# Decode attention and MLP: K and V in items of 32 pairs with a running maximum, instead of items of one KV head

## The chip, the core and the metric

The kernel runs on one core of one Trainium2 chip. The metric is the time of one execution on the device in microseconds (us). The core has five engines that run side by side, each with its own in-order instruction queue: TensorE (PE in the profile; its weight loads are PEld) does matrix products into PSUM, VectorE (DVE) and ScalarE (ACT) do elementwise work, reductions and 32x32 block transposes, GpSimd (POOL) does slower elementwise work, and SyncE (SP) issues transfers. Sixteen DMA engines carry the transfers from HBM into SBUF, the memory with 128 partitions from which the engines work.

## The reference

One token for each of 8 sequences goes through sliding-window attention and through an MLP, and a gate mixes both. With B = 8, D = 576, 32 query heads, 16 KV heads, head size 128, a cache of 8192 positions and a window of the last W = 2048:

```python
q = (x @ wq)                                   # (8, 32 heads, 128)
k = k_cache[:, :, Sk - W:, :]; v = v_cache[:, :, Sk - W:, :]   # each KV head serves 2 query heads
scores = einsum("bhqd,bhkd->bhqk", q, k) * Dh ** -0.5
a = einsum("bhqk,bhkd->bhqd", softmax(scores), v) @ wo
b = gelu(layernorm(x) @ w1 + b1) @ w2 + b2     # hidden size 4608
g = sigmoid((x * gate_w).sum(-1))
out = g * a + (1 - g) * b
```

All data are bf16. K and V of the window are 2 x 67 MB, which is most of what is read (154 MB); there are 128 pairs of sequence and KV head, and of each pair the window is 512 KB of K and 512 KB of V, contiguous.

## The kernel before

The kernel is written as a list of operations, each with an engine, its dependencies, an estimated cost and a priority. A small planner (class _Plan) simulates them with these costs and fixes from that the order on every engine; then each engine's instructions are emitted in that order, with semaphore waits for the dependencies. So an operation whose input is late holds up everything behind it on its engine.

Loading. Everything that is large is loaded on SP's queue in one order: wq and w1, then the entries of the list named stream, K0, K1, K2, V0, K3, V1 and so on up to V15, with a quarter of wo after every fourth V; then b2 and w2. SBUF has four slots of 32 KB a partition for K, V and w2, used in turn (take_slot: 1, 2, 0, 3), and half a slot more for wo. A load waits until the slot's earlier content has been read: for K the transposes, for V the weighted sum. The waits stand on SP in the order of the stream.

An item is one KV head of all 8 sequences, 4 MB (load_item). Its window is cut in 32 pieces of 64 positions; a row of 16 KB is one piece of one sequence, and a partition gets two rows.

Scores. For each item k_unit runs four times: a transpose of 128 x 2048 float32 on DVE (named tr, L647), which turns positions and head elements within 32x32 blocks (two bf16 at a time), into one of two KT buffers; then eight matmuls on PE (named qk, L659 and L175; one weight load serves four of them). A transpose waits for the qk that read its buffer two steps earlier. The weights qbd hold the query block-diagonally, and PSUM banks 0 to 3 collect the scores of two items, a group; there are eight groups. Entries that belong to no query are set to a large negative value beforehand (mask, L629, on ACT).

Softmax. Once per group: maximum over the scores (mx, L620, DVE), its combination over partitions (a tiny matmul, L622, and nb, L623), exp into P (L624, ACT, which also sums), the mask for the next group, transpose of P (pt, L631, DVE), and the sum's reciprocal through another tiny matmul.

Weighted sum. v_item issues 32 matmuls for an item (pv, L681): 32 columns of weights from the transposed P, 512 columns of V, two at a time in different column strips of the array. After each second item the result is masked and folded on DVE (vmul, acc), spread on POOL (ew), summed over partitions on PE (us), scaled on ACT (oev) and, after four items, transposed on DVE (oT). A projection with a quarter of wo follows on PE as soon as its chunk is there (class AccGroup, L563).

MLP and end. The hidden layer is computed at the start, beside the first K loads; its product with w2 comes last, in parts of 12, 12, 8, 3 and 1 rows of 128, with a few matmuls on zeros in between (keep_warm, L715). Then the accumulator is copied out by DVE and ACT (L777, L778) and stored.

Of the kernel before, what the change touches and what calls it, by code (L numbers as in the profile page):

```python
# [181 lines left out]
def build_kernel(nc, A_x, A_k_cache, A_v_cache, A_wq, A_wo, B_x, B_w1, B_b1, B_w2, B_b2, gate_w, out):  # L182
# [9 lines left out]
    HG = 2  # L192
    NG = Hkv // HG
# [16 lines left out]
    with ExitStack() as es:  # L210
# [20 lines left out]
        req("iqm", 32, F32)  # L231
        req("maskr", 4, F32)
        req("maskq", 4, F32)
        req("maskv", 4, F32)
        req("kq", 128, F32)
        req("selv", 128, F32)
        req("seln", 128, F32)
# [18 lines left out]
        req("sm", 32 * NG, F32)  # L256
        req("gcol", 1, F32)
        req("rr", 2, F32)
        req("on", 256, BF)
        req("EW", 512, F32)  # L260
        req("EV", 2 * 128, F32)
        req("oT", NG * 128, BF)
# [5 lines left out]
        over("vm", "uh", 0, 512, F32)  # L268
# [39 lines left out]
        iqm, maskr, selv = view("iqm"), view("maskr"), view("selv")  # L308
        maskq, maskv, kq = view("maskq"), view("maskv"), view("kq")
# [6 lines left out]
        qbd = view("qbd").rearrange("p (u h m) -> p u h m", u=4, h=4)  # L316
# [7 lines left out]
        sm = view("sm").rearrange("p (g k) -> p g k", g=NG)  # L324
        gcol = view("gcol")
        rr = view("rr")
        on = view("on")
        maskhd = view("maskhd")
        EW = view("EW").rearrange("p (g h d) -> p g h d", g=2, h=2)
        oT = view("oT").rearrange("p (i j c) -> p i j c", i=NG // 2, j=WOR)  # L330
        seln = view("seln")
# [4 lines left out]
        EV = view("EV").rearrange("p (u n) -> p u n", u=2)  # L336
        RAW = view("RAW")
        x_sb, gw_sb, y_bf = view("x_sb", 8), view("gw_sb", 8), view("y_bf", 8)
# [5 lines left out]
        def slot(s):  # L344
            return RAW[:, s * DE:min((s + 1) * DE, ND * DE + SE)]

# [21 lines left out]
        dma_keys = ["x", "b", "b2", "wq", "w1", "out"] + ["s%d" % i for i in range(ND + 1)] + ["t%d" % i for i in range(5)]  # L368
# [16 lines left out]
        o_mR = add("pool", lambda e: e.affine_select(out=maskR, in_=ones_bf, pattern=[[0, 128], [1, 4]], compare_op=ALU.is_equal,  # L385
                                                     fill=0.0, base=0, channel_multiplier=-1), deps=[o_ones], name="maskR", cost=0.8, prio=-1)
        o_mL = add("pool", lambda e: e.affine_select(out=maskL, in_=zeros_bf, pattern=[[0, 16], [1, 4], [0, 2]], compare_op=ALU.is_equal,
# [71 lines left out]
        o_iqm = add("dve", lambda e: e.tensor_reduce(out=iqm.rearrange("p (q m) -> p q m", q=4), in_=ident.rearrange("p (q r m) -> p q m r", q=4, r=4), axis=AXL.X, op=ALU.add), deps=[o_ident, o_obl], name="iqm", cost=0.3, prio=-1)  # L459
        o_maskr = add("dve", lambda e: e.tensor_reduce(out=maskr, in_=i32.rearrange("p (r m) -> p r m", r=4), axis=AXL.X, op=ALU.add), deps=o_i32, name="maskr", cost=0.2, prio=-1)  # L460
        o_maskq = add("dve", lambda e: e.tensor_reduce(out=maskq, in_=ident.rearrange("p (q m) -> p q m", q=4), axis=AXL.X, op=ALU.add), deps=[o_ident, o_xT], name="maskq", cost=0.3)
        o_kq = add("pool", lambda e: e.tensor_copy(kq.rearrange("p (q m) -> p q m", q=4), bass.AP(arena_f, offset=foffs("i32"), ap=[[AST // 2, 128], [0, 4], [1, 32]])), deps=o_i32, name="kq", cost=0.3, prio=-1)
        o_maskhd = add("dve", lambda e: e.tensor_reduce(out=maskhd, in_=iqm.rearrange("p (n h) -> p h n", h=2), axis=AXL.X, op=ALU.add), deps=[o_iqm], name="maskhd", cost=0.2, prio=-1)

        def seln_fn(e):
            dst = bass.AP(arena_f, offset=foffs("seln"), ap=[[AST // 2, 128], [32, 4], [8, 4], [1, 8]])
            src = bass.AP(arena_f, offset=foffs("i32"), ap=[[AST // 2, 128], [8, 4], [0, 4], [1, 8]])
            return e.tensor_copy(dst, src)
        o_seln = [add("pool", seln_fn, deps=o_i32, name="seln", cost=0.3, prio=-1)]
        o_selv = []  # L470
        for l in range(4):
            def selv_fn(e, l=l):
# [166 lines left out]
        def k_unit(i, s, d):  # L639
# [28 lines left out]
            if q == 3:  # L668
                softmax(g)
# [164 lines left out]
```

## Time and profile before

| what | value |
|---|---|
| median of 3 runs | 365.83 us (365.74 to 366.01) |
| profiled execution: its own time | 366.32 us |
| profiled execution: span, first to last instruction | 364.9 us |
| busy: PE, PEld, DVE, ACT, POOL | 247.1, 57.3, 217.0, 39.9, 23.3 us |
| mean granted TensorE clock | 0.846 |
| read from HBM | 154.31 MB, mean 423 GB/s over the span |
| time of the 16 DMA engines taken by SP's queue | 99.1% |

The page gives busy time per engine, the span in 40 slices of 9.1 us, the DMA queues, the chain of work that ended last (followed back from the last instruction to what released it), groups of instructions by source line, and transfers. In a line of the groups, "xN | busy us, mean ns | idle" means N instructions, their busy time, the mean of one, and how long the engine stood idle just before them with what ended that. Matmuls overlap, so their means are longer than their spacing. The granted clock is the share of full speed at which TensorE was allowed to run; it is either 1.0 or 0.5, in stretches that are multiples of 3.41 us.

### The profile page before, as it was taken

How to read it: one execution, taken by the hardware profiler on the slowest of the kernel's cores; microseconds unless marked ns; L12 is line 12 of the kernel's file. 1: busy time of each engine (PE TensorE's matmuls, PEld its weight loads, DVE VectorE, ACT ScalarE, POOL GpSimd, SP SyncE). 2: the span in 40 equal slices, each digit the busy share in tenths (PEclk: the TensorE clock that was granted, in tenths of full speed). 3: DMA queues.
4: the chain of work that ended last, by engine and by line, in shares of the span. 5: the costliest groups of instructions: out<-in, count | busy, mean ns of one | idle time of the engine just before them, and what ended most of it. 6: DMA issues, size and time to landing. Idle time of an engine off the chain costs nothing.

```text
span 364.9 us, 2626 instructions
## 1 busy us (share of the span) xinstructions
PE 247.1 (68%) x1347; PEld 57.3 (16%) x893; DVE 217.0 (59%) x160; ACT 39.9 (11%) x46; POOL 23.3 (6%) x66
## 2 busy tenths in 40 slices
PE   0355676599486957849297957868396938587776
PEld 0100000122111121202111121202110210102333
DVE  0723999667883757256675657276756667085220
ACT  1012100400310040000400040000400040001100
POOL 7210001000100000001000100001000100000000
PEclk9986599699769986969768986989589968969699
DMA  8999999999999999999999999999999999999996
GB/s 347 432 408 429 431 433 427 408 429 432 429 431 431 436 427 431 433 431 433 428 431 433 424 433 429 431 435 431 433 429 433 433 431 429 431 431 431 426 428 263
DMA packets 10674, 154.47 MB, mean 423 GB/s; under 512 B 764, under 2 KB 932, under 8 KB 1320
## 3 DMA queue, kind: packets, MB, share of 16 engines
q1 hardware_dynamic: 10608, 154.29, 99.1%
q8 instruction: 8, 0.13, 0.1%
q10 hardware_dynamic: 56, 0.03, 0.0%
q14 instruction: 2, 0.02, 0.0%
HBM read 154.31 MB, written 0.01 MB: 423 GB/s over the span
## 4 chain that ended last, share of the span: by engine, by line
DMA 66%; DVE 21%; PE 10%; issue 1%; ACT 1%; SPq 0%; DVEq 0%
DMA arena<-in_A_k_cache_dram 59%; DVE arena L647 20%; DMA arena<-in_B_w_dram 7%; PE ps L175 5%; PE ps L659 2%; PE ps L681 2%; DVE arena L546 1%; DVE arena L620 1%; ACT ps L629 1%; PE ps L563 0%; DVE arena L545 0%; PE ps L633 0%; DVE arena L777 0%; PE ps L622 0%; SPq L406 0%
## 5 line engine op out<-in xcount | busy, mean ns | idle before, releaser
L647 DVE STREAM_TRANSPOSE arena<-arena 128x2048 f32<-128x2048 f32 x64 | 144.1, 2289 | 61.8 <-DMA arena<-in_A_k_cache_dram 40.6
L175 PE MATMUL ps<-arena 128*128 128x512 bf16 (+2 forms) x454 | 135.0, 449 | 0.0
L659 PE MATMUL ps<-arena 128*128 128x512 bf16 x128 | 57.7, 451 | 52.5 <-DVE arena L647 52.5
L681 PE MATMUL ps<-arena 128*32 128x512 bf16 x512 | 60.3, 390 | 2.6 <-DVE arena L635 1.9
L624 ACT ACTIVATE arena<-ps,arena 128x2048 bf16<-128x2048 f32 x8 | 15.7, 1967 | 240.5 <-DVE arena L623 240.5
L659 PEld LDWEIGHTS ps<-arena 128*128 128x128 bf16 x128 | 14.0, 109 | 171.9 <-DVE arena L647 114.6
L681 PEld LDWEIGHTS ps<-arena 128*32 128x32 bf16 x512 | 25.2, 99 | 46.1 <-issue 20.3
L620 DVE TENSOR_REDUCE arena<-ps 128x1 f32<-128x2048 f32 x8 | 18.3, 2287 | 12.5 <-PE ps L175 12.4
L614 POOL COPY arena<-arena 32x128 bf16<-32x128 bf16 x32 | 9.2, 288 | 211.3 <-PE ps L175 201.5
L631 DVE STREAM_TRANSPOSE arena<-arena 128x2048 bf16<-128x2048 bf16 x8 | 18.3, 2292 | 6.4 <-ACT arena L624 6.4
L691 DVE SCALAR_TENSOR_TENSOR arena<-ps,arena 128x512 f32<-128x512 f32 x8 | 6.0, 751 | 19.8 <-PE ps L681 19.8
L563 PE MATMUL ps<-arena 128*8 128x288 bf16 (+1 forms) x140 | 12.6, 339 | 6.9 <-DVE arena L706 5.6
L700 PE MATMUL ps<-arena 128*128 128x256 f32 x16 | 5.8, 444 | 16.0 <-POOL arena L696 16.0
L633 PE MATMUL ps<-arena 128*128 128x1 f32 x16 | 4.6, 359 | 15.0 <-ACT ps L629 14.2
L629 ACT ACTIVATE ps<-arena 128x2048 f32<-128x2048 f32 x7 | 13.1, 1876 | 0.1
L696 POOL TENSOR_TENSOR arena<-arena 128x256 f32<-128x256 f32 x8 | 4.9, 612 | 111.3 <-DVE arena L623 63.3
L438 PE MATMUL ps<-arena 8*128 8x8 bf16 x8 | 0.6, 171 | 14.7 <-DVE arena L412 9.6
L694 DVE TENSOR_REDUCE arena<-arena 128x128 f32<-128x512 f32 x8 | 8.4, 1048 | 0.3
L563 PEld LDWEIGHTS ps<-arena 128*8 128x8 bf16 (+1 forms) x140 | 6.4, 97 | 13.5 <-DVE arena L706 7.0
L703 ACT ACTIVATE arena<-ps,arena 64x256 bf16<-64x256 f32 x8 | 3.7, 465 | 43.1 <-PE ps L700 43.1
L706 DVE STREAM_TRANSPOSE arena<-arena 128x256 bf16<-128x256 bf16 x4 | 2.5, 634 | 9.8 <-ACT arena L703 9.8
L541 DVE TENSOR_TENSOR arena<-arena 128x1152 f32<-128x1152 f32 x1 | 1.4, 1359 | 10.5 <-ACT arena L539 10.5
(88 smaller groups left out, 66.2 us busy)
## 6 DMA issues: line engine op xcount, KB each, us to landing
arena<-in_A_k_cache_dram SPq DMA_DIRECT2D x16, 4096.0 KB, 28.1
arena<-in_A_v_cache_dram SPq DMA_DIRECT2D x16, 4096.0 KB, 33.0
arena<-in_B_w_dram SPq DMA_DIRECT2D x1, 4608.0 KB, 23.4
arena<-in_A_wo_dram SPq DMA_DIRECT2D x4, 1152.0 KB, 34.7
arena<-in_A_wq_dram SPq DMA_DIRECT2D x1, 4096.0 KB, 13.0
arena<-in_B_w_dram SPq DMA_DIRECT2D x2, 1728.0 KB, 27.3
arena<-in_B_w_dram SPq DMA_DIRECT2D x1, 1152.0 KB, 26.7
arena<-in_B_w_dram SPq DMA_DIRECT2D x1, 576.0 KB, 24.3
```

The costliest lines, as they stand in the source:

```text
L175: return e.add_instruction(mybir.InstMatmult(name=nc.get_next_instruction_name(), engine=mybir.EngineType.PE, ins=[e.lower_ap(rhs), e.lowe ...
L563: ins = e.matmul(ps[32 * j:32 * j + 8, BK_ACC, 0:JN], lhsT, rhs[:, JN * j:JN * j + JN], start=False, stop=True, skip_group_check=True, til ...
L614: return e.tensor_copy(dst, src)
L620: mx = add("dve", lambda e: e.tensor_reduce(out=k(MX), in_=ps[:, 0:4, :].rearrange("p a n -> p (a n)"), axis=AXL.X, op=ALU.max), deps=[qk_ ...
L624: ex = add("act", lambda e: e.activation(out=Pm, in_=ps[:, 0:4, :].rearrange("p a n -> p (a n)"), func=ACTF.Exp, bias=k(NB), scale=SCALE, ...
L629: mask_done[g + 1] = add("act", lambda e: e.activation(out=ps[:, 0:4, :].rearrange("p a (n c) -> p (a n) c", c=4), in_=bass.AP(arena_f, of ...
L631: pt_done[g] = add("dve", lambda e: e.transpose(bass.AP(arena, offset=aoffs("PT") + 2048 * (g % 2), ap=[[AST, 128], [8, 64], [512, 4], [1, ...
L647: tr = add("dve", (lambda h=h, kb=kb: lambda e: e.transpose(bass.AP(arena_f, offset=foffs("KT") + kb * 2048, ap=[[AST // 2, 128], [1, 2048]]),
L659: mm = e.matmul(*args, start=False, stop=True, skip_group_check=True) if rc == 0 else held_matmul(nc, e, *args, stop=True, skip=True)
L681: mm = e.matmul(ps[c:c + 32, BK_OS[g % 2], :], PT[:, g % 2, 16 * c + 32 * t:16 * c + 32 * t + 32], slot(s)[:, (j % 2) * SE + 512 * t:(j % ...
L691: vmul = add("dve", lambda e: e.scalar_tensor_tensor(out=vmv, in0=ps[:, BK_OS[g % 2], :].rearrange("p (r d) -> p r d", r=4), scalar=rr[:, ...
L694: acc_ev[g] = add("dve", lambda e: e.tensor_reduce(out=EV[:, g % 2, :], in_=vm.rearrange("p (r d) -> p d r", r=4), axis=AXL.X, op=ALU.add) ...
```

## The change

An item is now a quarter of the window (512 positions) of 32 pairs of sequence and KV head, again 4 MB. The 512 positions of a pair are four rows of 32 KB that follow each other in HBM, and each partition gets one row. Four items make a group g of 32 pairs; there are four groups and 16 items n, as many as before.

- Softmax runs for every item, so 16 times instead of 8, with a maximum that runs over the four items of a group: nb takes the smaller of its own bound and the earlier one's, al is the factor by which earlier results shrink, ss the running sum. The scores of an item fill the four PSUM banks, and the mask is written for each. The combination over partitions is done once a group (sw, nbq, wt, rc, cf).
- For the weighted sum the transposed P is spread into a buffer with four diagonal blocks (ptx, 16 KB a partition, in the place of the half slot): four copies per item (qrx), two on POOL and two on ACT, and for the last item one on POOL, two on ACT, one on DVE. The buffer is cleared once (ptx0). Then 64 matmuls with 128 columns of weights and 256 columns of V run per item, after the scores of the next item in PE's order. There is one ptx buffer, so the copies of an item wait for the weighted sum of the item before.
- The result of an item is added to O on DVE (o): O = O x al + new. After the fourth item come vmul, acc, ew and us; oev and oT come once, at the very end.
- The stream is K0, K1, V0, K2, V1 and so on. All of wo is loaded after the last V, behind the first half of w2, and all of the projection follows it. The keep-warm matmuls are no longer called.
- Before the items, the masks and selection matrices are built in other shapes by small DVE and POOL instructions; the query copies on ACT are four of 256 elements instead of eight of 128.

The diff, cut to what the text speaks of (lines marked with - are the kernel before, those marked with + the new one):

```diff
-        NVW = Hkv // (Hq // WO_CH)
-        stream = [("K", 0), ("K", 1), ("K", 2)]
-        for vi in range(Hkv):
+        stream = [("K", 0), ("K", 1)]
+        for vi in range(NL):
             stream.append(("V", vi))
-            if (vi + 1) % NVW == 0:
...
+            if vi + 2 < NL:
+                stream.append(("K", vi + 2))
...
-        stream += [("B", 0)] + [("M", i) for i in range(len(M_CUTS))]
+        stream += [("B", 0), ("M", 0), ("W", 0), ("M", 1)]
 
...
-        slot_free = [[o_qp], [], [], [o_hp], [o_qp, o_hp]]
+        slot_free = [[o_qp], [], [], [o_hp]]
+        o_px0 = add("pool", lambda e: e.memset(ptx_f, 0.0), deps=[o_qp, o_hp], name="ptx0", cost=4.5)
...
-        def load_item(cache, nm, hkv):
+        def load_item(cache, nm, n):
             s = take_slot()
-            src = cache[:, hkv, S0:Sk, :].rearrange("b (x r) d -> x b (r d)", x=32)
-            d = dma("sp", lambda e: e.dma_start(slot(s).rearrange("p (u n) -> p u n", u=2), src), "s%d" % s, 8 * W * Dh * 2, deps=slot_free[s], name="%s%d" % (nm, hkv), after=last_dma[-1:])
+            g, i = divmod(n, 4)
+            src = cache.rearrange("b h s d -> (b h) s d")[32 * g:32 * g + 32, S0 + KL * i:S0 + KL * i + KL, :].rearrange("j (x r) d -> j x (r d)", x=4)
+            d = dma("sp", lambda e: e.dma_start(slot(s), src), "s%d" % s, 8 * W * Dh * 2, deps=slot_free[s], name="%s%d" % (nm, n), after=last_dma[-1:])
             last_dma.append(d)
...
+            mx = add("dve", lambda e: e.tensor_reduce(out=k(n, MX), in_=ps[:, 0:4, :].rearrange("p a n -> p (a n)"), axis=AXL.X, op=ALU.max), deps=[qk_unit[n]], name="mx%d" % n, cost=2.25, prio=5)
+            if i == 0:
+                nb = add("dve", lambda e: e.tensor_scalar(out=k(n, NB), in0=k(n, MX), scalar1=-SCALE, scalar2=None, op0=ALU.mult), deps=[mx], name="nb%d" % n, cost=0.16, prio=5)
+            else:
+                nb = add("dve", lambda e: e.scalar_tensor_tensor(out=k(n, NB), in0=k(n, MX), scalar=-SCALE, in1=k(n - 1, NB), op0=ALU.mult, op1=ALU.min), deps=[mx, nb_done[n - 1]], name="nb%d" % n, cost=0.16, prio=5)
...
+            ex = add("act", lambda e: e.activation(out=Pm, in_=ps[:, 0:4, :].rearrange("p a n -> p (a n)"), func=ACTF.Exp, bias=k(n, NB), scale=SCALE, accum_out=k(n, S)),
+                     deps=[nb, pt_done[n - 1] if n else o_zz], name="exp%d" % n, cost=1.95, prio=5)
...
+            if n + 1 < NL:
+                mask_done[n + 1] = add("act", lambda e: e.activation(out=ps[:, 0:4, :].rearrange("p a (n c) -> p (a n) c", c=32), in_=bass.AP(arena_f, offset=foffs("maskv"), ap=[[AST // 2, 128], [0, 64], [1, 32]]), func=ACTF.Copy),
+                                       deps=[ex], name="mask%d" % (n + 1), cost=1.85, prio=4)
...
+            pt_done[n] = add("dve", lambda e: e.transpose(bass.AP(arena, offset=aoffs("PT") + 2048 * (n % 2), ap=[[AST, 128], [1, 2048]]), Pm),
+                             deps=[ex] + (px_done[n - 2] if n >= 2 else [o_yTp, o_hT]), name="pt%d" % n, cost=2.3, prio=5)
+            if i:
+                al_done[n] = add("act", lambda e: e.activation(out=k(n, AL), in_=k(n - 1, NB), func=ACTF.Exp, bias=k(n, NB), scale=-1.0), deps=[nb], name="al%d" % n, cost=0.25, prio=4)
+                ss_done[n] = add("dve", lambda e: e.scalar_tensor_tensor(out=k(n, SS), in0=k(n - 1, SS if i > 1 else S), scalar=k(n, AL), in1=k(n, S), op0=ALU.mult, op1=ALU.add),
+                                 deps=[ex, al_done[n], ss_done.get(n - 1)], name="ss%d" % n, cost=0.16, prio=3)
...
+                sw_pe = add("pe", lambda e: e.matmul(ps[:, BK_S, 4:5], swp, k(n, NB), start=True, stop=True), deps=[nb, o_u] + o_swp + prev, name="sw_pe%d" % g, cost=0.5, prio=3)
+                nbq = add("dve", lambda e: e.tensor_tensor(out=G(NBQ), in0=k(n, NB), in1=ps[:, BK_S, 4:5], op=ALU.min), deps=[sw_pe], name="nbq%d" % g, cost=0.16, prio=3)
...
+                sw = add("dve", lambda e: e.tensor_tensor(out=G(SW), in0=k(n, SS), in1=G(WT), op=ALU.mult), deps=[wt, ss_done[n]], name="sw%d" % g, cost=0.16, prio=3)
+                su = add("pe", lambda e: e.matmul(ps[:, BK_S, 0:1], pair, G(SW), start=True, stop=True), deps=[sw, o_pair] + prev, name="sum_pe%d" % g, cost=0.5, prio=3)
+                rc = add("dve", lambda e: e.reciprocal(out=G(RC), in_=ps[:, BK_S, 0:1]), deps=[su], name="rc%d" % g, cost=0.16, prio=3)
+                cf = add("dve", lambda e: e.tensor_tensor(out=G(CF), in0=G(WT), in1=G(RC), op=ALU.mult), deps=[rc], name="cf%d" % g, cost=0.16, prio=3)
+                grp_done[g] = [nbq, rc, cf]
...
+                    m = 4 * n + 2 * rh + hh
+                    kb = m % 2
+                    deps = [d] + ([qk_half[m - 2]] if m >= 2 else [o_selp])
+                    tr = add("dve", (lambda rh=rh, hh=hh, kb=kb: lambda e: e.transpose(bass.AP(arena_f, offset=foffs("KT") + kb * 2048, ap=[[AST // 2, 128], [1, 2048]]),
...
+            qk_unit[n] = qk
...
+            softmax(n)
...
+        def v_item(n):
+            s, d = load_item(A_v_cache, "dv", n)
...
+            ob_ = BK_OS[n % 2]
+            px_done[n] = []
+            for c in range(4):
+                def fn(e, c=c):
+                    dst = bass.AP(arena, offset=32 * c * AST + PX + 32 * c, ap=[[AST, 32], [128, 64], [1, 32]])
...
+                    if px_engs[n][c] == "act":
+                        return e.activation(out=dst, in_=src, func=ACTF.Copy)
+                    return e.tensor_copy(dst, src)
+                px_done[n].append(add(px_engs[n][c], fn, deps=[pt_done[n], pv_done.get(n - 1), o_px0], name="qrx%d_%d" % (n, c), cost={"act": 1.8, "dve": 2.2, "pool": 4.0}[px_engs[n][c]], prio=5))
...
             def pv_fn(e):
                 mm = None
-                for t in range(16):
-                    for j in (i - 1, i):
-                        c = 32 * (j % 4)
-                        mm = e.matmul(ps[c:c + 32, BK_OS[g % 2], :], PT[:, g % 2, 16 * c + 32 * t:16 * c + 32 * t + 32], slot(s)[:, (j % 2) * SE + 512 * t:(j % 2) * SE + 512 * t + 512],
-                                      start=(t == 0), stop=(t == 15), skip_group_check=True, tile_position=(0, c))
+                for r in range(64):
+                    rhs = bass.AP(arena, offset=aoffs("RAW") + s * DE + 128 * r, ap=[[AST, 128], [SE, 2], [1, 128]])
+                    mm = e.matmul(ps[:, ob_, 0:256], ptx[:, r, :], rhs, start=(r == 0), stop=(r == 63), skip_group_check=True)
                 return mm
...
+            deps = [d, o_u] + px_done[n] + [o_done.get(n - 2)]
+            pv = add("pe", pv_fn, deps=deps, name="pv%d" % n, cost=7.2, after=pv_hist[-1:] + [qk_unit.get(n + 1)])
...
+            if i == 0:
+                o_done[n] = add("dve", lambda e: e.tensor_copy(Oc, ps[:, ob_, 0:256]), deps=[pv, acc_done.get(g - 1)], name="o%d" % n, cost=0.4, prio=6)
+            else:
+                o_done[n] = add("dve", lambda e: e.scalar_tensor_tensor(out=Oc, in0=Oc, scalar=al, in1=ps[:, ob_, 0:256], op0=ALU.mult, op1=ALU.add), deps=[pv, al_done[n], o_done[n - 1]], name="o%d" % n, cost=0.5, prio=6)
+            if i == 3:
+                vmv = vm.rearrange("p (r d) -> p r d", r=2)
...
+                           deps=[o_done[n], o_maskrh, o_hf] + grp_done[g], name="vmul%d" % g, cost=0.5, prio=6)
...
+        def wo_all(_):
+            def place(s, at, i):
+                dst = slot(s)[:, at:at + WO_CH * D]
+                h0 = WO_CH * i
+                d = dma("sp", lambda e: e.dma_start(dst, A_wo[128 * h0:128 * (h0 + WO_CH), :].rearrange("(p j) c -> p (j c)", j=WOR)),
+                        "o%d" % i, WO_CH * 128 * D * 2, deps=slot_free[s] if at == 0 else [], name="d_wo%d" % i, after=last_dma[-1:])
+                last_dma.append(d)
+                dj = dst.rearrange("p (j c) -> p j c", j=WOR)
+                return AccGroup("proj%d" % i, [(oT[:, j, i, :], dj[:, j, :]) for j in range(WOR)], o_T + [d], cost=1.0, prio=1).op
+            s = take_slot()
+            done = [place(s, WO_CH * D * i, i) for i in range(3)]
+            slot_free[s] = done
+            s = take_slot()
+            done = [place(s, 0, 3)]
+            m2_at.append((s, WO_CH * D))
+            slot_free[s] = done
+
+        m2_at = []
         o_m2 = []
 
```

## The prediction

> **What bounds the kernel now.** Of the page I read the slices and queues first, then the chain, then the groups; after that the chain in order of time, and windows of the TensorE clock.
>
> ```profile
> GB/s 347 432 408 429 431 433 427 408 429 432 429 431 431 436 427 431 433 431 433 428 431 433 424 433 429 431 435 431 433 429 433 433 431 429 431 431 431 426 428 263
> ...
> q1 hardware_dynamic: 10608, 154.29, 99.1%
> ...
> DMA 66%; DVE 21%; PE 10%; issue 1%; ACT 1%; SPq 0%; DVEq 0%
> ...
> L647 DVE STREAM_TRANSPOSE arena<-arena 128x2048 f32<-128x2048 f32 x64 | 144.1, 2289 | 61.8 <-DMA arena<-in_A_k_cache_dram 40.6
> ...
> L681 PE MATMUL ps<-arena 128*32 128x512 bf16 x512 | 60.3, 390 | 2.6 <-DVE arena L635 1.9
> L624 ACT ACTIVATE arena<-ps,arena 128x2048 bf16<-128x2048 f32 x8 | 15.7, 1967 | 240.5 <-DVE arena L623 240.5
> ...
> L620 DVE TENSOR_REDUCE arena<-ps 128x1 f32<-128x2048 f32 x8 | 18.3, 2287 | 12.5 <-PE ps L175 12.4
> ```
> The transfers are the bound: the queue is 99.1% busy at about 431 GB/s, and the transposes wait for K (40.6 us). So 4.19 MB take 9.73 us and a pair (one K and one V transfer) 19.45. The question is whether the engines still fit under 19.45 us a pair. What one step takes, from the chain in order of time and a timeline of TensorE:
>
> ```profile
> 37.31 2.31 DVE arena L647
> ...
> 49.63 8.79 DVE arena L647 x4
> ...
> 68.51 0.45 PE ps L659
> 68.96 1.28 PE ps L175 x3
> ...
> 78.61 0.22 PE ps L659
> 78.84 0.69 PE ps L175 x3
> ...
> 361.26 1.73 PE ps L563 x24
> ```
> ```profile
> 23.19 0.61 PE L510 MATMUL ps<-arena 128*128 128x256 bf16 x4 [2.60 <-DVE arena L504]
> ```
> Four transposes in a row take 8.8 to 9.0. One weight load and four matmuls of 512 columns take 1.71 at half clock and 0.91 at full clock. Four pairs of weight load and 256-column matmul took 0.61 with a mean of 275 ns each: (610 - 275) / 3 = 112 ns apart at full clock. The windows are 3.41 us long; columns are PE busy, count, granted clock, DMA share, GB/s:
>
> ```profile
> 116.42:119.83 3.41, 1.82 (x8) 1.00 0.95 408
> ...
> 194.93:198.34 3.41, 1.67 (x8) 1.00 1.04 447
> 198.34:201.75 3.41, 3.17 (x8) 0.56 1.01 432
> 201.75:205.17 3.42, 2.92 (x13) 0.94 0.97 414
> ...
> 297.32:300.74 3.42, 1.77 (x14) 0.50 1.01 431
> 300.74:304.15 3.41, 2.59 (x7) 0.50 1.00 428
> 304.15:307.56 3.41, 2.81 (x12) 0.94 0.98 413
> ```
> A window with 1.67 busy is followed by half clock, one with 1.82 was not; a half-clock window with 2.59 busy ends it, one with 1.77 does not. About half a window decides.
>
> **The change, part by part.** Transfers: same bytes. In windows of the trace the 32 KB rows of wq run at 428 GB/s (4 to 14 us), the 36 KB rows of w1 at 438 (16 to 24 us), the 16 KB rows of K and V at 431 (100 to 300 us). For the 134 MB of K and V that is between 2.2 us lost and 5.0 gained; I take 0, as wq's rows have the new size. The rows now come from 32 pairs 2 MiB apart; no row of this trace has such a pitch, and it is a rival below. Every K item now has its own maximum, exp, mask and transpose of P, where two items shared one of each: on DVE that adds 8 x (2.29 + 2.29) = 37 us. The weighted sum has 64 matmuls of 256 columns an item with full 128-column weights, for 32 of 512 that ran two at a time (3.56 us in the chain). A pair then has DVE 9.0 + 2.29 + 2.29 + some 0.9 = 14.5, ACT 2.16 + 1.88 + 0.2 + two spreading copies (at most 1.97 each, as exp) = 8.2, PE 32 x 0.227 + 64 x 0.112 = 14.4. None fills 19.45; the order does it.
>
> In the changed program's order DVE runs, per pair n: four transposes, mx, nb, pt, o(n-1), ss, then the transposes of n+1. PE runs the four halves qk(n), then all of pv(n-1). So o(n-1) stands ahead of the next transposes and waits for a weighted sum that starts only after the last qk. Nothing of this depends on a transfer once K and V lie in their slots. The ring: transposes 9.0, last half 0.05 + 1.98 (8 x 0.227 and the drain), pv 64 x 0.112 + 0.2 = 7.35, o about 0.5 (0.75 for 512 columns), ss 0.17, gaps 0.15: 19.2 at full clock. The other branch, mx 2.29, nb 0.25, exp 2.2, pt 2.3, is 7.05 instead of 7.35, hidden by pv. pv could also pay its weight load whole: 112 + 109 = 221 ns each, 14.1 us; I take 112, since that row is the same pair of instructions.
>
> Each group of four adds the normalisation: sw, rc, cf between transposes (0.5), nbq (0.2), vmul and acc (0.4 + 0.6) ahead of the transposes: 1.7.
>
> The clock: from pv's end to the next qk, PE idles for o, ss and the first transpose, 3.1 us. Wherever the windows' edges fall, one holds nearly 1.55 us of idleness or more; unless the edge splits the gap almost evenly (0.3 of 3.41) busy is under 1.7 and half clock follows for one window of qk. A half then takes 3.4 instead of 1.8, and the transpose that needs its buffer waits: first half 2.3 to 5.7, third transpose to 8.0, fourth to 10.2, last half done at 12.2, against 11.0. So about 1.0 a pair, with bounds 0 and 2.2 (two halves at half clock).
>
> By the Trainium skill (TensorE: Matmul & The Clock Gate, Part 1), half clock comes back after a whole idle window of about 3.4 us; 3.1 us would not trip it, and the ring would stay at its full-clock sum, the second rival below. The windows differ: 1.67 busy was already too little.
>
> Start: K0 lands at 37.3 as before and its transposes end at 49.6, with the MLP's DVE work between. Then mx0 to 54.2, exp 56.6, mask 58.6. PE has idled 7 us, so qk(1) starts cold: K1's third and fourth transposes end at 64.3 and 67.7, qk(1) at 69.7, pv(0) at 77.0. Here the order takes the next first transpose ahead of pt, which saves 2.3 and the PE gap: K2's other three start at 77.8, K3's at 94.9. The first of K4 starts at 112.3, and K4 has landed at 47.0 + 3 x 19.45 = 105.4: 7 us behind.
>
> From K4 to K15: 11 periods of 19.2 = 211.2; groups 3 x 1.5 and 2 x 0.2 = 4.9; less 2.3 (K10's first transpose stands early again, which also closes PE's gap there); clock in the other ten, 10.0: together 223.8, or 20.3 a pair against 19.45. K15 starts at 336.1; it landed at 319.3.
>
> Tail from there: last half 12.0, pv14 19.4, spreading by ACT (2 x 1.9) 23.2, pv15 30.6, o, vmul, acc 32.2, ew 32.9, us 33.7, oev 34.2, oT 34.9, the projection's 64 matmuls at 72 ns (1.73 / 24) 39.6, w2's last 24 41.3, output copy 0.45 and its store 1.44 (364.9 - 363.46): 43.2. Span 379.3, +14.4. The profiled run took 366.32, 1.42 over its span; the median of the runs is 365.83, 0.5 less. So 379.3 + 0.9 = 380.
>
> What I cost at nothing: POOL's two copies a pair are 1.9 each by slope (128 elements 288 ns, 512 606 ns) or 4.6 by the short row x 16; between one pv's end and the next start lie 11.8, so 9.2 is covered. Its clearing of the spread buffer (4096 float32; L393 cleared 2048 bf16 in 1.8, so 3.6 by elements and 7.2 by bytes) starts when h is through, about 32, and is needed at 59. On SP, Wo's four loads stood behind every fourth V and now stand behind w2's first half, so three of them move past 22, 14 and 6 loads of K and V: 10.0 MB (23.3 us) follow the last V instead of 6.5 MB (15.1). They wait for K15's transposes (346.3) and pv14 (355.5), about when the queue gets there; the projection wants them only from 371. If the ring were shorter, these 23.3 us would be the cover of the tail: it holds while K15 starts by 364.9 - 43.2 = 321.7. PE's m2 half of 1.7 ahead of pv15 lies in the spreading's time. The keep-warm matmuls are gone; w2's matmuls stand in their place.
>
> **Rivals.** (1) The transfers still set the end, the faster side. K15 must start by 321.7, so 11 periods in 209.4, 19.0 each with everything, from the same start. For it: four transposes took 8.8 once. Against: 19.2 before groups and clock. It gives 364.9, less up to 5.0 from the rows and 1.0 from the two slices at 408 (2 x 9.1 x 23 / 431): a span of 358.9 to 364.9, so 360 to 366. (2) The clock stays full: 380 - 11 = 369. (3) The 2 MiB pitch slows reads: it decides below 134 MB in 16 x 20.3 us, 413 GB/s. No row has this pitch; at the first slice's 347 GB/s K and V cost 75 us more than at 431: 440. The Trainium skill (DMA: Bandwidth & Descriptors, Latency and other measured facts) gives 164 GB/s at a row pitch of 2 MiB against 214 in full for copies within HBM; by that ratio, an estimate, 330 GB/s and about 460. No run here shows it. (4) pv pays weight loads: at the bound, 14.1 instead of 7.15, twelve sums and the last pay 7 each, 470; at a fifth of that 398. Against it stands the one row with this pair of instructions.
>
> **How the numbers follow.** Ring with half clock, 374 to 392: 0.52. (2), 366.6 to 374: 0.18. (1): 0.17, of it 0.13 faster by over 0.2% (below 365.1) and 0.04 within 0.2%, about what a measurement tells apart. (3): 0.07. (4): 0.06, half of it below 400. Slower: 0.83. The range 364 to 400 leaves out some 0.08 of (1) below and 0.1 above.
>
> **What would show it.** DVE's transposes waiting for PE more than for K; DMA share falling behind only near the end; o waiting for pv; half-clock windows once a pair; pv at 7.3; the last landing some 10 us ahead of the end. I am wrong if the transposes wait for K until the end, if pv takes over 8, or if K lands at more than 19.6 apart.

## The result and the profile after

| | before | after |
|---|---|---|
| median of 6 runs | 365.89 us (365.72 to 366.13) | 392.36 us (390.15 to 398.22) |
| ratio, 95% interval | | 1.0702 (1.0671 to 1.0732) |
| busy: PE, DVE, ACT, POOL in the profiled run | 247.1, 217.0, 39.9, 23.3 us | 294.0, 271.4, 131.6, 78.2 us |

The change made the kernel 26.5 us slower by the medians. Two of the six runs of the changed kernel, the profiled one among them, were slow, and the ratio goes by fast runs alone (390.15 to 392.65 us), which makes 25.7 us. The profiled run took 398.22 us, 5.9 above the median, with a granted clock of 0.884 where most others have 0.895 to 0.912. So periods and times at half clock read from it are a little long; the durations of single steps are not.

From the page of the changed kernel, the slices, the queue, the chain and the groups that answer to those shown of before:

```profile
GB/s 356 419 449 421 423 427 452 436 426 421 429 447 436 429 421 416 427 438 437 376 426 362 416 304 418 423 433 375 419 393 389 423 343 414 340 399 336 403 71 1
...
q1 hardware_dynamic: 6512, 154.29, 92.4%
...
PE 58%; DVE 35%; ACT 3%; DMA 2%; issue 1%; POOL 0%; ACTq 0%
...
L665 DVE STREAM_TRANSPOSE arena<-arena 128x2048 f32<-128x2048 f32 x64 | 145.4, 2294 | 21.3 <-PE ps L175 21.2
...
L706 PE MATMUL ps<-arena 128*128 128x256 bf16 x1024 | 115.7, 274 | 0.0
...
L699 POOL COPY arena<-arena 32x2048 bf16<-32x2048 bf16 x31 | 58.4, 1884 | 251.9 <-PE ps L706 162.9
...
L642 DVE SCALAR_TENSOR_TENSOR arena<-arena 128x1 f32<-128x1 f32 x12 | 16.6, 1379 | 0.0
L717 DVE SCALAR_TENSOR_TENSOR arena<-arena,ps 128x256 f32<-128x256 f32 x12 | 5.8, 481 | 8.7 <-PE ps L706 8.0
...
L720 DVE SCALAR_TENSOR_TENSOR arena<-arena 128x256 f32<-128x256 f32 x4 | 5.7, 1428 | 0.1
```

The transfers have left the chain (DMA 66% before, 2% now). Up to the 19th slice they run as fast as before; later the slots come free late, and the transfers have gaps. The transposes no longer wait for K but for PE (21.2 us, none of it for DMA). So the ring through DVE and PE sets the time, as forecast. The line that was not forecast is L642. It is ss, the running sum, one number a partition, and it takes 1.38 us in the mean. Its sister L628 (nb) has the same form and takes 159 ns.

The chain of waits of the changed kernel, in order of time (start, length, what), over one period:

```profile
254.84 7.00 PE ps L706 x64
261.84 0.02 issue
261.87 0.48 DVE arena L717
262.35 1.51 DVE arena L642
263.86 2.23 DVE arena L665
266.09 0.05 issue
266.14 0.61 PE ps L677
266.75 1.28 PE ps L175 x3
...
277.08 7.00 PE ps L706 x64
```

This is the forecast ring, weighted sum, o, ss, transpose, with 1.5 us where 0.17 stood. PE's gap from 261.84 to 266.14 is 4.3 us instead of 3.1, and the qk that follows runs at half clock (1.28 for three matmuls, 0.68 at full clock). What stands beside L642 on POOL is seen in the timeline of VectorE and of POOL around an earlier item, and around the end of a group (start, length, engine, line, idle before and what ended it):

```profile
76.61 0.43 DVE L715 COPY arena<-ps 128x256 f32<-128x256 f32 x1
76.95 1.65 DVE L642 SCALAR_TENSOR_TENSOR arena<-arena 128x1 f32<-128x1 f32 x1
78.53 2.30 DVE L665 STREAM_TRANSPOSE arena<-arena 128x2048 f32<-128x2048 f32 x1
```
```profile
76.71 3.83 POOL L699 COPY arena<-arena 32x2048 bf16<-32x2048 bf16 x2 [13.22 <-PE ps L706]
```
```profile
136.03 0.48 DVE L717 SCALAR_TENSOR_TENSOR arena<-arena,ps 128x256 f32<-128x256 f32 x1
...
136.13 1.88 POOL L699 COPY arena<-arena 32x2048 bf16<-32x2048 bf16 x1 [17.85 <-PE ps L706]
136.55 1.74 DVE L720 SCALAR_TENSOR_TENSOR arena<-arena 128x256 f32<-128x256 f32 x1
...
158.78 0.21 DVE L642 SCALAR_TENSOR_TENSOR arena<-arena 128x1 f32<-128x1 f32 x1
158.89 3.83 POOL L699 COPY arena<-arena 32x2048 bf16<-32x2048 bf16 x2 [17.49 <-DVE arena L715]
...
384.19 0.48 DVE L720 SCALAR_TENSOR_TENSOR arena<-arena 128x256 f32<-128x256 f32 x1
```

ss starts at 76.95, POOL's first copy has run since 76.71, and ss ends at 78.60, when that copy ends (76.71 + 1.88 = 78.59). vmul (L720) starts at 136.55 beside a copy that ends at 138.01, and takes 1.74. At 158.78 ss happens to start 0.1 us before POOL, and takes 0.21; after the last item POOL has no copy, and vmul takes 0.48. Both have two inputs in SBUF. The transposes, with one input, run beside the same copies at their usual length. o (L717), with one of its inputs in PSUM, starts 0.1 us ahead of the copies here, so its length shows nothing; e6 below does. The weighted sum's end releases all of them at once, the copies because the spread buffer comes free, o because its operand is there; so the collision comes once a period.

By the Trainium skill (SBUF — State Buffer, Who interferes with whom), a VectorE instruction with two SBUF inputs contends with a GpSimd instruction that reads SBUF, and the one that starts first holds the shared port for its whole length. The trace agrees where POOL starts first; e6 below has the other order. It also agrees that a GpSimd instruction that only writes does not count: the product L548 (two SBUF inputs) lies at 33.88 beside POOL's clearing of the spread buffer (32.74, 3.51 long) and takes 1.36 us, as the like L550 does without it. One input alone does not spare every VectorE instruction, though. L549, which scales by one constant and adds another, takes 1.60 us beside the same clearing, where the like of the kernel before (L542) takes 0.76; and the last item's spreading copy on VectorE takes 2.02 beside POOL's, where e6 has 0.69.

### The profile page after: what moved, and what is told of

Its sections match the earlier page's. It is cut to its first block, busy times and chain, and to the rows that moved or that the text cites. A ratio compares the mean times of both kernels' runs of the same rounds, so it can differ in the third digit from the quotient of the medians.

```text
span 397.0 us, 3760 instructions
## 1 busy us (share of the span) xinstructions
PE 294.0 (74%) x1826; PEld 128.9 (32%) x1379; DVE 271.4 (68%) x203; ACT 131.6 (33%) x107; POOL 78.2 (20%) x78
## 3 DMA queue, kind: packets, MB, share of 16 engines
q1 hardware_dynamic: 6512, 154.29, 92.4%
## 4 chain that ended last, share of the span: by engine, by line
PE 58%; DVE 35%; ACT 3%; DMA 2%; issue 1%; POOL 0%; ACTq 0%
PE ps L706 29%; DVE arena L665 23%; PE ps L175 19%; PE ps L677 7%; DVE arena L642 4%; DMA arena<-in_gate_w_dram 2%; PE ps L570 2%; DVE arena L720 1%; DVE arena L717 1%; ACT arena L698 1%; PE ps L492 1%; DVE arena L553 1%; DVE arena L624 1%; ACT arena L630 1%; ACT ps L634 0%
## 5 line engine op out<-in xcount | busy, mean ns | idle before, releaser
L665 DVE STREAM_TRANSPOSE arena<-arena 128x2048 f32<-128x2048 f32 x64 | 145.4, 2294 | 21.3 <-PE ps L175 21.2
L706 PE MATMUL ps<-arena 128*128 128x256 bf16 x1024 | 115.7, 274 | 0.0
L706 PEld LDWEIGHTS ps<-arena 128*128 128x128 bf16 x1024 | 100.8, 99 | 26.0 <-issue 12.1
L699 POOL COPY arena<-arena 32x2048 bf16<-32x2048 bf16 x31 | 58.4, 1884 | 251.9 <-PE ps L706 162.9
L630 ACT ACTIVATE arena<-ps,arena 128x2048 bf16<-128x2048 f32 x16 | 31.5, 1967 | 199.7 <-DVE arena L628 145.8
L677 PEld LDWEIGHTS ps<-arena 128*128 128x128 bf16 x128 | 14.3, 111 | 186.5 <-DVE arena L665 118.0
L698 ACT ACTIVATE arena<-arena 32x2048 bf16<-32x2048 bf16 x32 | 61.0, 1906 | 10.8 <-PE ps L706 9.9
L624 DVE TENSOR_REDUCE arena<-ps 128x1 f32<-128x2048 f32 x16 | 36.6, 2289 | 31.4 <-PE ps L175 31.4
L638 DVE STREAM_TRANSPOSE arena<-arena 128x2048 bf16<-128x2048 bf16 x16 | 36.9, 2307 | 25.5 <-ACT arena L630 25.5
L634 ACT ACTIVATE ps<-arena 128x2048 f32<-128x2048 f32 x15 | 28.1, 1872 | 0.1
L642 DVE SCALAR_TENSOR_TENSOR arena<-arena 128x1 f32<-128x1 f32 x12 | 16.6, 1379 | 0.0
L717 DVE SCALAR_TENSOR_TENSOR arena<-arena,ps 128x256 f32<-128x256 f32 x12 | 5.8, 481 | 8.7 <-PE ps L706 8.0
L548 DVE TENSOR_TENSOR arena<-arena 128x1152 f32<-128x1152 f32 x1 | 1.4, 1357 | 11.3 <-ACT arena L546 11.3
L720 DVE SCALAR_TENSOR_TENSOR arena<-arena 128x256 f32<-128x256 f32 x4 | 5.7, 1428 | 0.1
## 6 DMA issues: line engine op xcount, KB each, us to landing
arena<-in_B_w_dram SPq DMA_DIRECT2D x1, 4608.0 KB, 23.3
arena<-in_A_wq_dram SPq DMA_DIRECT2D x1, 4096.0 KB, 12.9
```

Of the source, the lines that this page charges most:

```text
L624: mx = add("dve", lambda e: e.tensor_reduce(out=k(n, MX), in_=ps[:, 0:4, :].rearrange("p a n -> p (a n)"), axis=AXL.X, op=ALU.max), deps=[ ...
L630: ex = add("act", lambda e: e.activation(out=Pm, in_=ps[:, 0:4, :].rearrange("p a n -> p (a n)"), func=ACTF.Exp, bias=k(n, NB), scale=SCAL ...
L634: mask_done[n + 1] = add("act", lambda e: e.activation(out=ps[:, 0:4, :].rearrange("p a (n c) -> p (a n) c", c=32), in_=bass.AP(arena_f, o ...
L638: pt_done[n] = add("dve", lambda e: e.transpose(bass.AP(arena, offset=aoffs("PT") + 2048 * (n % 2), ap=[[AST, 128], [1, 2048]]), Pm), deps ...
L642: ss_done[n] = add("dve", lambda e: e.scalar_tensor_tensor(out=k(n, SS), in0=k(n - 1, SS if i > 1 else S), scalar=k(n, AL), in1=k(n, S), o ...
L665: tr = add("dve", (lambda rh=rh, hh=hh, kb=kb: lambda e: e.transpose(bass.AP(arena_f, offset=foffs("KT") + kb * 2048, ap=[[AST // 2, 128], ...
```

## Experiments

Two theories stood at first. A, the lock: ss and vmul wait for POOL's copies; their excess is (16.6 - 12 x 0.2) + 3 x 1.26 = 18 us of DVE's ring. B, the clock: PE's idle gaps give half clock, and ss's length is a side matter. Times are compared with runs of the kernel before on the same chip (365.67 for the first four kernels, 365.84 for the next four, 365.92 for the last two).

**ss ahead of o** (e1). POOL's copies stay where they are; ss is done before they start, in all items but the last.

```diff
-... name="o%d" % n, cost=0.5, prio=6)
+... name="o%d" % n, cost=0.5, prio=6, after=[ss_done.get(n + 1)])
```

> The changed kernel with one edit: on DVE the running sum ss of an item stands before the accumulation o of the item before, not behind it, so it no longer meets POOL's copies. (The planner then also puts K10's first transpose in its usual place, which costs up to 2.3 us.) Theory A, VectorE's ss waits until POOL's copy is through: ss takes 0.2 instead of 1.6 us, eleven pairs save 1.4 each, and the shorter gap on TensorE saves up to 4 more: 373 to 379 us against about 392. Theory B, ss is slow of itself or waits for ScalarE's factor, and the excess over the forecast is half clock alone: 389 to 395 us.

Measured: 377.53 us (376.94 to 378.16), ratio 1.0325 (1.0308 to 1.0342), 14.8 less than the changed kernel. L642 takes 306 ns in the mean, 3.7 us in all, of which 1.73 are the last item's; so ss itself is 12.9 us shorter. The rest is the net of a shorter gap on PE (half clock from 60 us to 50 us ahead of the end: 37.4 us for 61.9) and of K10's first transpose, which is back in its usual place. A holds. VectorE's timeline of this kernel, with the ring's new period of 19.6:

```profile
250.20 0.18 DVE L642 SCALAR_TENSOR_TENSOR arena<-arena 128x1 f32<-128x1 f32 x1
250.35 0.48 DVE L717 SCALAR_TENSOR_TENSOR arena<-arena,ps 128x256 f32<-128x256 f32 x1
250.74 4.50 DVE L665 STREAM_TRANSPOSE arena<-arena 128x2048 f32<-128x2048 f32 x2
...
270.36 2.30 DVE L665 STREAM_TRANSPOSE arena<-arena 128x2048 f32<-128x2048 f32 x1
```

**Zeros behind every weighted sum but the last two** (e2): 28 matmuls on zeros fill PE's gap; the lock stays.

```diff
+            if n + 2 < NL:
+                fills[n + 2] = fill(n, pv)
...
+                for k in range(28):
+                    args = (ps[:, BK_S, 8:256], zeros_bf, maskR[:, 0:248])
```

> The changed kernel with 28 matmuls on zeros (248 columns, into unused columns of a PSUM bank) behind each weighted sum but the last two, about 2.9 us of the 4.3 us that TensorE idles there. If half clock costs what the trace of the changed kernel shows (transposes idle 1.35 us a pair for TensorE): no half-clock windows in the steady stretch and 375 to 381 us. If half clock costs 1.0 a pair as forecast: 381 to 383. If the clock hides behind the lock (theory A alone explains everything): 388 to 395. ss stays at 1.6 us in all three.

Measured: 384.44 us (383.98 to 389.61), ratio 1.0543 (1.0477 to 1.061). Half clock in the same stretch falls from 61.9 us to 9.4, and ss stays at 1379 ns. The time is in none of the three ranges expected; it lies between the second and the third. So filling the gap is worth 6 (by the ratios) to 8 us (by the medians), less than the lock; part of what it gained is lost to the zeros' own place, as in e4.

**All copies on ACT** (e3). ss and vmul stay behind o, where they were; the engine of two copies an item changes, for all items but the last. With the other costs the planner also moves a few things on DVE: K10's first transpose is back in its usual place, and sw, rc and cf of three groups stand one transpose later.

```diff
-        px_engs = [("pool", "pool", "act", "act")] * (NL - 1) + [("pool", "act", "act", "dve")]
+        px_engs = [("act", "act", "act", "act")] * (NL - 1) + [("pool", "act", "act", "dve")]
```

> The changed kernel with all four spreading copies of an item on ScalarE (but for the last item), none on GpSimd. Theory A: ss falls to 0.2 and vmul to 0.5 us although they stand where they stood, 15 + 4 us less, and the copies' 7.6 us a pair still fit into the 11.8 us between two weighted sums: 371 to 378 us. Theory B: ss stays at 1.6 us, and ScalarE has 3.8 us a pair more: 390 to 400 us.

Measured: 373.88 us (373.16 to 376.39), ratio 1.0235 (1.0197 to 1.0273). From the groups of this kernel:

```profile
L642 DVE SCALAR_TENSOR_TENSOR arena<-arena 128x1 f32<-128x1 f32 x12 | 2.5, 212 | 0.0
L720 DVE SCALAR_TENSOR_TENSOR arena<-arena 128x256 f32<-128x256 f32 x4 | 1.9, 485 | 0.1
```

The two groups fell by 14.1 and 3.8, together 17.9 us, and the time by 18.5 (17.1 by the ratios). That these are so close is partly chance: half clock falls too (31.0 us), while ACT now has four copies of 1.9 in a row (3% of the chain for 1%) and K10's first transpose no longer stands early. For the lengths of ss and vmul this is the cleanest look at the lock: both behind o as before, and no reader on POOL.

**ss ahead of o, and 24 zeros** (e4).

> Both edits, ss early and 24 matmuls on zeros behind a weighted sum. If lock and half clock are the two terms that lengthen the ring beyond its full-clock sum of 19.2 us, they add up: 366 to 371 us, near the 369 of the second rival, with the last landing within 6 us of the end. If something else holds the ring: above 374 us.

Measured: 377.32 us (376.12 to 378.69), ratio 1.0318 (1.029 to 1.0345): no gain over e1, against the expectation. Where the ring ran undisturbed at full clock its period was 18.3 (first transposes at 156.52 and 174.86). But the zeros stood ahead of the tiny matmul of the group's maximum (sw_pe), and nbq stands ahead of the next transposes on DVE. From the timelines of VectorE and of PE of this kernel:

```profile
113.60 0.48 DVE L720 SCALAR_TENSOR_TENSOR arena<-arena,ps 128x256 f32<-128x256 f32 x1
116.26 0.15 DVE L650 TENSOR_TENSOR arena<-arena,ps 128x1 f32<-128x1 f32 x1 [2.18 <-PE ps L649]
116.33 4.50 DVE L666 STREAM_TRANSPOSE arena<-arena 128x2048 f32<-128x2048 f32 x2
```
```profile
113.40 0.27 PE L744 MATMUL ps<-arena 128*128 128x248 bf16 x1
113.50 2.60 PE L175 MATMUL ps<-arena 128*128 128x248 bf16 x23
115.94 0.28 PE L649 MATMUL ps<-arena 128*128 128x1 f32 x2
```

That is 2.2 us in three of the groups, and 1.7 twice at the start, where the next transpose was already done and only the zeros stood in front of its qk.

**The zeros put where they delay nothing** (e5): none behind the first two weighted sums, and behind sw_pe in every third item of a group; they also write to another PSUM bank. ss stands ahead of o as in e4.

```diff
+            if 2 <= n < NL - 2:
+                fills[n + 2] = fill(n, pv)
...
+            return add("pe", fn, ..., after=[pv] + ([sw_ops[n // 4]] if n % 4 == 2 else []), prio=9)
```

> ss early and 24 matmuls on zeros as in the combined run, but none behind the first two weighted sums, where the next transpose stands early and TensorE has no gap, and in every group's last item behind the small matmul sw that VectorE's nbq waits for. In the combined run the zeros cost 1.7 us twice and 2.2 us three times there. If they hid the gain of the full clock, this one is at 366 to 370 us (377.3 less 10). If a full clock is worth little in this ring, it stays at 374 to 378.

Measured: 367.14 us (366.28 to 369.37), ratio 1.0042 (1.0024 to 1.0059). Half clock is down to 2.1 us (37.4 in e1), and the time is 10.4 us below e1: that is what the clock costs, at the least, once the lock of ss is away. It may be more, as K12 and K15 already wait for their transfers here (landings at 261.55 and 319.59, first transposes at 261.57 and 319.61).

**The order alone** (e6): no zeros, POOL keeps its copies. The ring is opened instead: ss ahead of o, the next item's first transpose ahead of the transpose of P, and o(n-1) behind the next item's second transpose.

```diff
+                    if rh == 0 and hh == 0 and 1 <= n <= 15:
+                        pt_done[n - 1].after.append(tr)
+                    if rh == 0 and hh == 1 and n >= 2:
+                        o_done[n - 2].after.append(tr)
...
+... name="o%d" % n, cost=0.5, prio=6, after=[ss_done.get(n + 1)])
```

> The changed kernel with another order on VectorE and nothing else: ss ahead of o; the first transpose of the next item ahead of pt; o of the item before behind the second transpose of the next item. So the transposes no longer wait for the weighted sum. If the ring through o is what holds the changed kernel, the period of the engines falls to some 16.4 us a pair (mx, nb, first transpose, pt, ss, second transpose, o, third and fourth, last qk), below the 19.45 of the transfers, the lag of 7 us at K4 is made up, and the end is set by the transfers: 364 to 367 us, DMA share near 1 to the end. If TensorE's work or GpSimd's and ScalarE's copies hold it: above 372 us.

Measured: 366.55 us (365.79 to 368.64), ratio 1.0028 (1.0012 to 1.0043): 25.8 of the 26.5 us are back with three instructions a pair moved on one engine. Some 11 of them are the opened ring (against e1, which moves ss alone); in these is vmul, which no longer meets a copy (0.48 us). From the page of this kernel, the slices, the queue and the chain, and behind them two pieces of its chain in order of time:

```profile
GB/s 347 431 434 408 456 413 446 424 438 429 431 440 420 449 416 451 414 447 417 442 427 433 438 424 443 424 445 422 445 420 436 421 445 418 442 434 421 420 423 200
...
q1 hardware_dynamic: 6512, 154.29, 98.3%
...
DMA 46%; DVE 34%; PE 14%; ACT 3%; issue 3%; POOL 0%; ACTq 0%
```
```profile
293.49 26.30 DMA arena<-in_A_k_cache_dram
319.79 0.02 issue
319.81 2.31 DVE arena L665
...
363.16 0.45 DVE arena L814
```

The transfers set the pace again, up to the landing of K15 at 319.8; the tail of 45.3 us behind it ends the run. The last slice moves 200 GB/s where it moved 263 before, as the transfers now end a little ahead of the engines.

The timelines of VectorE and of POOL of this kernel also show what the changed one could not:

```profile
92.85 3.83 POOL L703 COPY arena<-arena 32x2048 bf16<-32x2048 bf16 x2 [12.20 <-DVE arena L642]
94.94 0.44 DVE L721 SCALAR_TENSOR_TENSOR arena<-arena,ps 128x256 f32<-128x256 f32 x1
...
341.61 0.69 DVE L703 COPY arena<-arena 32x2048 bf16<-32x2048 bf16 x1
341.64 2.41 POOL L703 COPY arena<-arena 32x2048 bf16<-32x2048 bf16 x1 [13.42 <-PE ps L648]
```

o (L721) starts at 94.94, behind the start of POOL's second copy (about 94.8), and takes 0.44 us, no longer than elsewhere: with one input in PSUM it does not wait. At 341.61 VectorE's own spreading copy starts 0.03 us ahead of POOL's and takes 0.69, and POOL's takes 2.41 instead of 1.88. In the changed kernel POOL was first there (370.36), and VectorE's copy took 2.02. So the one that starts first holds up the other.

**The order, K and V as two halves of 16 KB** (e7).

> The same with each row of 32 KB read as two of 16 KB (eight pieces a pair, two rows a partition), so the same bytes to other partitions in twice the packets; the values of K and V then lie with other partitions, so the result of the attention is another one, and the work is the same. Where the transfers set the end, it shows what the length of the rows is worth: nothing by the forecast (less than 1 us apart from the run with 32 KB rows), up to 5 us slower by the fastest rows of the kernel before, up to 2 us faster by wq's rows.

Measured: 366.34 us (366.06 to 369.67), ratio 1.0029 (1.0009 to 1.0048). The expectation is wrong in one thing: both halves of a row go to the same partition in the same order, so the computation is unchanged. They are also neighbours in HBM, and the queue counts 6512 packets, as with rows of 32 KB. So this was the same transfer written otherwise, and it tells nothing of the length of rows; it repeats e6.

**The order only up to item 12** (e8): the first transpose goes ahead of P's transpose only for n up to 12 (`1 <= n <= 12`).

> The order of e6, but from item 13 on the first transpose of the next item stands behind pt again, so the last items go through with less delay. If the run with the new order ends by the transfers, this one is equal to it within 0.5 us; if it ends by the engines after the last V, 1 to 3 us faster.

Measured: 366.52 us (366.4 to 369.57), ratio 1.0037 (1.0019 to 1.0054), the same as e6: DVE's order in the last items does not decide the end.

**The order, and rows that are 16 KB** (e9). A partition gets two rows of 16 KB from places 64 KB apart.

```diff
-            src = cache.rearrange("b h s d -> (b h) s d")[...].rearrange("j (x r) d -> j x (r d)", x=4)
-            d = dma("sp", lambda e: e.dma_start(slot(s), src), ...)
+            src = cache.rearrange("b h s d -> (b h) s d")[...].rearrange("j (u x r) d -> u j x (r d)", u=2, x=4)
+            for u in range(2):
+                d = dma("sp", lambda e, u=u: e.dma_start(slot(s)[:, u * SE:u * SE + SE], src[u]), ...)
```

> This is the kernel with the three steps put ahead of the accumulation (e6_order, 366.55), with K and V read in rows of 16 KB: each item comes as two transfers of 2 MB, and a partition gets two rows of 16 KB that lie 64 KB apart in HBM, so they cannot be joined into one row of 32 KB as those of e7_order_16kb were (its queue counted 6512 packets, as many as with 32 KB rows; so e7 was a repetition of e6 and tells nothing of rows). K and V are permuted alike, so the computation is unchanged. The packets should go from 6512 to about 10608, as before the change. Theory A (row length is worth nothing, the prediction's term of 0): 366.0 to 367.2. Rival B (the longer rows win some of the 5.0 us that the best window allowed, and the order's cost eats it): 368 to 372. Rival C (longer rows cost): 364 to 365.6.

Measured: 367.75 us (367.19 to 369.68), ratio 1.0037 (1.0019 to 1.0055), with 11120 packets. This is between the two ranges expected. Its interval overlaps that of e6, which ran on another chip, and its medians lie 1.8 above the kernel before where e6's lie 0.7 above. So 32 KB rows are worth at most about 1 us here, and that includes the 16 more K and 16 more V transfers of this kernel; whether they are worth anything stays open.

**The order, and all copies on ACT** (e10): the edit of e3 on top of e6.

> This is the kernel with the three steps put ahead of the accumulation (e6_order, 366.55), with POOL's two copies of an item moved to ScalarE (all items but the last). If the transfers alone set its end, as the even 423 GB/s says, taking the lock of POOL away from the small DVE steps (L642 338 ns in the mean in e6, 0.21 alone) gains nothing and the later start of the weighted sum (four copies of 1.9 in a row, 3.8 later) costs nothing: 366 to 367. If what is left over the kernel before (0.7 us) is the lock still, 365 to 365.9. If the branch from the transpose of P over the copies to the weighted sum is the next bound, above 368.

Measured: 366.56 us (365.81 to 369.4), ratio 1.0024 (0.9997 to 1.005). Moving the copies gains nothing that can be told from no change, which fits transfers that set the time. It says nothing of the lock, though: L642 has 338 ns in the mean in both kernels. In both that is one long instance, the last item's ss (1.73 us), which stands beside the one copy that stays on POOL; the other eleven take about 0.2. None of the kernels beat the one before.

## Why the prediction was right and wrong

The forecast was 380 in a range of 364 to 400, 0.83 on slower; 392.36 is inside the range and slower. The mechanism, a ring through o that no transfer holds, was right: e6 opens it by order alone and has 366.55. The size was not: +14 forecast, +26.5 measured. That the time lies inside the range is in part luck: the forecast's own case, the ring with half clock, ended at 392, and the room from there to 400 held little more than the milder half of weight loads in pv (0.03), which fell. A lock that the prediction did not price brought the time there.

- **The step that failed is "ss 0.17", and with it "vmul and acc (0.4 + 0.6)"**, together with the sentence that POOL's copies are covered. They are covered in time, between one weighted sum and the next, as written (1884 ns each, 1.9 forecast). But they start at the moment when ss and vmul are due and hold these up for 1.3 to 1.4 us. Two operations were priced each by its own row, and not the pair of them. e3 has this at 17 to 18 us. Without it the changed kernel takes 373.9 (e3) to 377.5 (e1, where vmul still waits), so the rest of the sum was too long by 2.5 to 6.
- **The full-clock ring**, 19.2 forecast, was 18.3 where it ran undisturbed in e4, without ss. The weighted sum took 7.00 instead of 7.35 (the 112 ns apart from one row of before were right: 7.00 / 64 = 109), the four transposes 8.81 instead of 9.0, ss (0.17) stands elsewhere, and the rest is in gaps. So the ring at full clock would hardly have held the kernel: in e5 the eleven periods from K4 to K15 took 211.0 us (108.64 to 319.61), 19.2 each with the groups and waits for transfers in them, and the transfers need 19.45. It takes the lock or half clock to put the ring above them.
- **pv and pt as branches of equal length** was right: at 261.80 the transpose of P is done, at 261.84 the weighted sum.
- **Half clock, 10.0 in all**: e5 against e1 has at least 10.4 for a gap of 2.80 us. With the lock the gap is 4.3 in the period shown, and half clock follows for longer (61.9 us in 13 spells after, 37.4 in 10 in e1, counted from 60 us to 50 us ahead of the end; the 61.9 are of the long profiled run, whose granted clock is lower than that of most others). In e2 filling that gap gives 6 to 8.
- **The clock rule weighed in the prediction.** In e1 PE stands idle from 250.3 to 253.1, and then 3.4 us at half clock follow (254.5 to 257.9):

```profile
253.10 0.40 PE L677 MATMUL ps<-arena 128*128 128x512 bf16 x1 [2.80 <-DVE arena L665]
```

No window of 3.41 us fits in that gap, and the one ahead of the half clock (251.05 to 254.46) has PE busy for 1.36 us; so a whole idle window, as the Trainium skill (TensorE: Matmul & The Clock Gate, Part 1) asks, is not needed; the prediction's row of 1.67 busy was the better guide.
- **The start**: K4's first transpose at 112.3 forecast, 116.3 measured; three times ss's excess of 1.4 lies ahead of it, and K0's transposes ended 0.9 late.
- **From K4 to K15**: 223.8 forecast, 234.8 in the profiled run, of which up to 5.9 are that run's own length over the median.
- **The tail**: 43.2 forecast, 45.8 measured. The last weighted sum took 8.34 for 7.35 and the last 88 matmuls 7.25 for 6.35 (4.6 + 1.73), both partly at half clock.
- **POOL's clearing**: 3.51 us at 32.74, about as by elements (3.6). It was not free, as the prediction had it: L549 beside it took 0.8 longer, so K0's first transpose started at 38.18, 0.6 behind K0's landing (37.60), and K0's transposes ended at 50.5 instead of 49.6.
- **The rivals.** (1), the transfers still set the end: not for this kernel, whose DMA share fell; it holds as soon as the ring is opened, at 366.5, and nearly so with half clock filled, at 367.1. (2), full clock throughout: fell with the half clock in the chain. (3), slow reads at a pitch of 2 MiB between pairs: fell. From the second slice on the profile shows 416 to 452 GB/s until the slots come late, and e6 has 423 over the whole run, as before; the lower figure that the Trainium skill (DMA: Bandwidth & Descriptors, Latency and other measured facts) has at this pitch is for copies within HBM, and does not hold for these loads. (4), whole weight loads in pv: fell, 109 ns a pair of load and matmul.
- **What would show it**: transposes that wait for PE, slots that come late and half clock once a period were there. That DMA falls behind only near the end was not: it falls behind from the middle, as a period took 21.3 in the profiled run (234.8 / 11), 1.9 over the transfers' 19.45 instead of 0.9. The last landing is 17 us ahead of the end (380.0 of 397.0), not 10.

## To carry to other kernels

When two operations are released by the same event, price them together: an instruction on VectorE with two operands in SBUF, or a plain copy of the kind here, waits for a GpSimd copy that has just started, so a sum of one column can cost as much as the copy. "Covered" work on another engine must be looked at for what it holds, not only for whether it fits in time. And before a change is given up, look at the order on the engine that closes the ring: moving three instructions a pair gave back 25.8 of 26.5 us here.

## What was unexpected

A VectorE operation on 128 x 1 elements went from 0.21 to 1.6 us beside a GpSimd copy of 1.88 us, while transposes, and o with one operand in PSUM, kept their length beside such copies. But a VectorE copy with one SBUF operand did not (2.02 us for 0.69), nor did POOL's copy when VectorE's came first (2.41 for 1.88). An idle gap of 2.80 us on TensorE was followed by 3.4 us at half clock, and spells of half clock follow in 9 of the 11 periods from K4 to K15 of e1; the kernel before has more half clock (81.9 us from 60 us to 50 us ahead of the end, 61.9 after) and lost nothing by it, as its transfers set the pace.
